# Gate and output stage of a transformer block: transposed squares in ScalarE's queue, output products a product later, another start and end

## The chip, the cores and the metric

The kernel is one program on 1 core of one Trainium2 chip. The metric is device time in microseconds (us); before the change it was 1758.81 us, the median of 3 runs (1757.84 to 1760.7). Beside it stands one profiled execution with a trace of every instruction. Engines are named as in the profile: PE is TensorE's matmul, PEld its weight load, DVE VectorE, ACT ScalarE, POOL GpSimd, SP SyncE. SPq and ACTq rows are an engine's sequencer issuing a DMA. The profile puts "PE" for a matmul and marks the granted clock of TensorE as PEclk.

## What is computed

A pre-norm attention block is followed by a gated MLP; x is 2048 rows of 512, with 32 heads:

```python
h  = x + attention(layernorm(x))                  # 32 heads of 16, softmax
z  = gelu(layernorm(h) @ w_in)                    # 2048 x 1376
z1 = z[:, :688]; z2 = layernorm(z[:, 688:])
g  = w_sp @ z2 + b_sp                             # w_sp is 2048 x 2048, over the rows
y  = h + (z1 * g) @ w_out                         # w_out is 688 x 512
```

The change touches the last two lines only.

## The kernel before

The first 1454 us of the profiled execution are attention, h and z (lines 1 to 1280); the change leaves their instructions alone, but for one small memset on POOL that stands elsewhere. What follows is called the **gate stage** here, lines 1286 to 1565, under a manual schedule: every engine runs its instructions in the order in which the code writes them.

The 2048 output rows are eight pairs of 128-row blocks, p = 0 to 7 (block p and block p + 8). For one p, `w_sp @ z2` is done with seven block products instead of eight, by sums of blocks; they are called b11, t1, t2, b22, t3, b21, n4 after their right operand, and come in that order. Each `product` (line 1299) is 24 matmuls: 8 blocks of 128, each as three fp16 matmuls for fp32 precision (`mm3`, lines 108 to 110). The left operands (256 KB pairs, tile `op`) are fetched eight products ahead from DRAM scratch by SP: `ask`, line 1162, one after every product. Three PSUM tiles A, C, B take the sums:

- A takes b11, is drained by ACT into `p1`, takes t2 on top, is drained by ACT into `v`, takes t3 on top, is read by DVE (`br`), takes n4 on top, is read by DVE (`bl`).
- C takes t1, is drained by ACT into `q5`, takes b22 on top, is read by DVE (`right`).
- B takes b21 and is read by DVE (`left`).

The four pieces of g * z1 (two row blocks, left half and right half of the 688 columns) are put into tile `pr`, multiplied by z1 on POOL (lines 1512, 1520, 1537) or DVE, levelled by a power of two (`level`, DVE; `raise_`, ACT line 1361). "Half 1" is the right columns, ready after t3, "half 0" the left columns, ready after n4.

For the product with w_out, pr has to be transposed. For p = 0 to 6 that is done without PE: DVE transposes 32 x 32 squares within partitions (`squares`, lines 1375 to 1381), SP sends the 384 KB to DRAM scratch (`send`, line 1384), SP brings them back in four DMAs of 96 KB with the squares in their places (`bring`, line 1392), ACT rounds to fp16 (`hi`, line 1398), DVE takes the rest (`lo`, lines 1407 to 1413), and PE multiplies with w_out (`multiply`, line 1437: 16 matmuls of 512 columns for half 1, 18 for half 0, both row blocks). DVE adds the result to h (`gather`, line 1452) and SP stores it (line 1455). The last p transposes on PE instead (`turn`, line 1423; `split`, lines 1431 to 1435).

All this is written out in the loop of line 1480: while p is in its products, the transposed half 1 of p - 1 is multiplied after t1, and its half 0 after b22. Here M1 and M0 stand for these two multiplications. SP's order in a loop turn is: bring of half 1, fetch of z1 and h of the next p (`fetch`, line 1465), operator loads, send and bring of half 0, stores, send of half 1.

At the stage's start SP fetches z1 and h of p = 0, then w_out (`raw_w`, line 1475), and for p = 0 DVE measures w_out's largest entry after t1 (`weigh_w`, line 1321), PE spreads it over the partitions by a matmul with ones after t2 (`measure_w`, line 1327), and ACT and DVE make its fp16 parts (lines 1332 and 1333). The tiles of the stage come from pools `fin_1` and `fin_2`, laid on memory that the pools of the z stage used: a first tile has to wait until the last reader of the old tile under it is done.

Of the kernel before, what the change touches and what calls it, by code (L numbers as in the profile page):

```python
# [19 lines left out]
P = 128  # L20
# [39 lines left out]
def block_kernel(ctx: ExitStack, tc: tile.TileContext, x, wqkv, wo, w_in, w_sp4, b_sp, w_out, out):  # L60
# [1225 lines left out]
    with ExitStack() as fin:  # L1286
        f1 = fin.enter_context(tc.tile_pool(name="fin_1", bufs=1))
# [49 lines left out]
        class Rows:  # L1337
# [45 lines left out]
            def send(self, half):  # L1383
                nc.sync.dma_start(t_scr[2 * (self.p % 2) + half],
                                  self.turned[half].rearrange("p q w i a -> p (q w i a)"))

            def bring(self, half):

                t = self.turned[half] = f2.tile([P, 4, 2, 3, 32], F32, name="whole")
                src = t_scr[2 * (self.p % 2) + half].rearrange("(j b) (q c) -> q b j c", j=4, q=4)  # L1390
                for q in range(4):
                    nc.sync.dma_start(t[32 * q:32 * q + 32].rearrange("b j w i a -> b j (w i a)"), src[q])
# [66 lines left out]
        def fetch(p):  # L1459

            got = []
            for name, src, n in (("z1", z_scr, FH), ("h", h_scr, D)):
                for i in range(2):
                    t = f2.tile([P, n], F32, name=f"{name}{i}", bufs=2 + (name == "h"))
# [4 lines left out]
        with tc.manual_schedule(engines={E.PE, E.Activation, E.DVE, E.Pool, E.SP}):  # L1469
# [4 lines left out]
            nxt = fetch(0)  # L1474
            nc.sync.dma_start(raw_w[:, :5, :], w_out[:5 * P, :].rearrange("(i p) c -> p i c", p=P))
            for r0 in (TW - fn, P - fn):
                nc.sync.dma_start(raw_w[r0:r0 + fn, 5, :], w_out[5 * P:, :])
            now = None
            for p in range(HB):
# [5 lines left out]
                p1, v, q5 = [f2.tile([P, FC], F32, name=n) for n in ("p1", "v", "q5")]  # L1485
# [3 lines left out]
                product(A, "b11")  # L1489
                if p:  # L1490
                    before.send(0)
                nc.scalar.activation(p1, A, AF.Identity, bias=bt)  # L1492
                product(C, "t1")
                nc.scalar.activation(q5, C, AF.Identity, bias=bb)
# [10 lines left out]
                if p:  # L1505
                    for w in range(2):
                        before.gather(1, w, accs[w])
                else:
                    measure_w()
# [20 lines left out]
                if last:  # L1530
                    for w in range(2):
# [65 lines left out]
```

## Time and profile before

| | us |
|---|---|
| median of 3 runs | 1758.81 |
| profiled execution | 1767.72 |
| its span, first to last instruction | 1765.94 |
| gate stage, first b11 matmul (1454.36) to the span's end | 311.58 |
| PE busy in the gate stage | 270.12 |
| DVE, ACT, POOL busy in it | 111.03, 48.63, 32.55 |

The stage is read by loop turns: a turn runs from the first matmul of its b11 to the first of the next one. A row of a stretch table reads: stretch, its length, busy time and number of instructions of each engine, granted clock of TensorE, share of the DMA engines, GB/s. A row of a timeline reads: start, duration, engine, line, operation, out<-in, shape, count, and in brackets the engine's idle time before it and what ended it. A row of the waits reads: who, for whom, total, how often, longest. In the chain a row of a DMA runs from its issue to its landing.

### The profile page before, as it was taken

To read this page: it belongs to the slowest core of one execution; us is meant where nothing else is said; L and a number is where in the kernel's file an instruction comes from. 1 tells how busy PE (TensorE), PEld (TensorE's weight loads), DVE (VectorE), ACT (ScalarE), POOL (GpSimd) and SP (SyncE) were. 2 spreads that over 40 slices of the span, in tenths; PEclk is the share of its full clock that TensorE was granted. 3 is DMA by queue.
4 is the path that set the end of the run, shared out by engine and by line. 5 is a ranking of instruction groups with operands and counts; after the bars stand their busy time and mean duration, and the time that the engine had idled before them with its cause. 6 is when DMAs were issued, how large, how long until landed. Compare 5 with 4: busy or idle time off the path is not lost.

```text
span 1765.9 us, 36677 instructions
## 1 busy us (share of the span) xinstructions
PE 1713.9 (97%) x13499; PEld 645.4 (37%) x13499; DVE 1450.7 (82%) x3051; ACT 1317.7 (75%) x2584; POOL 813.5 (46%) x1062
## 2 busy tenths in 40 slices
PE   9999999999999999999999999999999997988998
PEld 4433222222222222222222222222246664545554
DVE  7688999999999999999999999999567873323334
ACT  4335999999999999999999999999965452111111
POOL 1322777766760388667776776000026762000000
PEclk9999999999999999999999999999999998999999
DMA  5534333332320244435444344001145535656461
GB/s 179 159 101 141 92 87 86 100 92 61 103 50 19 70 123 120 135 109 144 138 123 132 115 140 107 13 13 32 38 118 146 171 132 194 210 167 205 159 196 47
DMA packets 194013, 201.53 MB, mean 114 GB/s; under 512 B 66824, under 2 KB 142920, under 8 KB 193832
## 3 DMA queue, kind: packets, MB, share of 16 engines
q1 hardware_dynamic: 191528, 193.54, 38.2%
q10 hardware_dynamic: 2304, 5.64, 0.8%
q8 instruction: 106, 1.74, 0.4%
q14 instruction: 75, 0.61, 0.1%
HBM read 127.61 MB, written 71.44 MB: 113 GB/s over the span
## 4 chain that ended last, share of the span: by engine, by line
PE 70%; DVE 15%; DMA 6%; POOL 2%; issue 2%; ACT 2%; SPq 2%; ACTq 0%; DVEq 0%; POOLq 0%
PE pv L829 25%; PE s L804 17%; PE m L224 9%; DVE mx L229 7%; PE acc L108 3%; PE acc L110 3%; PE acc L109 3%; PE g L108 3%; PE g L110 3%; PE g L109 3%; DMA t_scr<-squares 2%; DMA rc<-r_scr 2%; DVE ab L238 1%; DVE og L839 1%; DVE rs_t L125 1%
## 5 line engine op out<-in xcount | busy, mean ns | idle before, releaser
L813 ACT ACTIVATE pt<-s 128x512 f32<-128x512 f32 x1968 | 1006.2, 637 | 4.9 <-PE m L224 3.7
L229 DVE TENSOR_REDUCE mx<-m 128x1 f32<-128x512 f32 x1510 | 947.8, 683 | 12.6 <-PE m L224 3.9
L804 PE MATMUL s<-qst,kst 50*128 50x512 f16 x2048 | 604.3, 379 | 0.2
L829 PE MATMUL pv<-pt,vst 128*32 128x256 f32 (+1 forms) x6056 | 598.1, 466 | 4.1 <-DVE og L839 1.3
L224 PE MATMUL m<-kst,qst 48*128 48x512 f16 x1510 | 452.5, 381 | 0.0
L804 PEld LDWEIGHTS <-kst 50*128 50x128 f16 x2048 | 132.0, 94 | 352.0 <-issue 322.9
L829 PEld LDWEIGHTS pv<-pt,vst 128*32 128x32 f32 x6056 | 119.5, 108 | 290.1 <-issue 276.7
L224 PEld LDWEIGHTS <-qst 48*128 48x128 f16 x2048 | 159.2, 93 | 173.7 <-issue 124.5
L224 PE MATMUL m<-uvs,qst 48*128 48x512 f16 x504 | 190.5, 380 | 0.0
L238 DVE CUSTOM_DVE_ANT_0 ab<-m,ab 128x512 f32<-128x512 f32 x252 | 170.7, 677 | 2.7 <-ACT ab L234 2.7
L246 POOL TENSOR_SCALAR nm<-nm 128x16 f32<-128x16 f32 x32 | 6.5, 204 | 359.8 <-DVE nm L243 359.8
L234 ACT ACTIVATE ab<-m 128x512 f32<-128x512 f32 x252 | 157.3, 624 | 16.5 <-PE m L224 15.8
L1361 ACT ACTIVATE pr<-pr,up 128x304 f32<-128x304 f32 (+1 forms) x32 | 17.0, 574 | 138.8 <-DVE up L1315 138.8
L990 POOL TENSOR_TENSOR op<-raw,op 128x512 f16<-128x512 f32 x80 | 92.7, 1159 | 6.1
L913 POOL TENSOR_TENSOR raw<-raw 128x512 f32<-128x512 f32 (+1 forms) x84 | 83.1, 989 | 6.7
L918 POOL TENSOR_TENSOR acc_sp<-acc_sp,raw 128x512 f32<-128x512 f32 x63 | 80.3, 1275 | 4.5
L108 PE MATMUL acc<-wi,hT 128*128 128x344 f16 x256 | 79.1, 309 | 1.4 <-ACT hT L99 1.4
L110 PE MATMUL acc<-wi,hT 128*128 128x344 f16 x256 | 79.1, 309 | 0.3 <-DVE hT L105 0.3
L109 PE MATMUL acc<-wi,hT 128*128 128x344 f16 x256 | 79.1, 309 | 0.0
L1512 POOL TENSOR_TENSOR pr<-pr,z 128x344 f32<-128x344 f32 x8 | 9.7, 1215 | 143.4 <-issue 81.4
L108 PE MATMUL g<-t,op 128*128 128x344 f16 x192 | 60.6, 316 | 4.4 <-ACT p L1492 4.4
L910 POOL TENSOR_SCALAR raw<-raw 128x512 f32<-128x512 f32 (+1 forms) x88 | 52.1, 592 | 19.7 <-DMA raw<-in_wqkv 12.4
(247 smaller groups left out, 2247.4 us busy)
## 6 DMA issues: line engine op xcount, KB each, us to landing
raw<-in_w_sp SPq DMA_DIRECT2D x128, 256.0 KB
s_scr<-op SPq DMA_DIRECT2D x64, 256.0 KB
op<-s_scr SPq DMA_DIRECT2D x32, 512.0 KB
a_scr<-op SPq DMA_DIRECT2D x48, 256.0 KB
op<-a_scr SPq DMA_DIRECT2D x24, 512.0 KB
o_scr<-og SPq DMA_DIRECT2D x64, 128.0 KB
qst<-q_scr SPq DMA_DIRECT2D x192, 32.0 KB
kst<-k_scr SPq DMA_DIRECT2D x48, 128.0 KB
```

Of the source, the lines that this page charges most:

```text
L108: nc.tensor.matmul(ps, lh, rh, start=first, stop=False, **kw)
L109: nc.tensor.matmul(ps, lh, rl, start=False, stop=False, **kw)
L110: nc.tensor.matmul(ps, ll, rh, start=False, stop=last, **kw)
L224: nc.tensor.matmul(acc, q[r, p, c], keys[r, p], start=True, stop=True)
L229: nc.vector.reduce_max(at(t, e if t else e - 1), acc, axis=AX.X)
L234: nc.scalar.activation(ab[0], acc, AF.Abs)
L238: nc.vector.tensor_tensor_reduce(ab[0], acc, ab[0], 0.5, LOW, ALU.add, ALU.max, at(0, 0))
L804: nc.tensor.matmul(s, kst[hg % 2][r, p, kb * P:(kb + 1) * P], qst[hg * NQ + qb][r, p, :], start=True, stop=True)
L813: nc.scalar.activation(pts[p, kb][:, t, :], s, AF.Exp, scale=scales_[hg // 2])
L829: nc.tensor.matmul(pv[0][32 * j:32 * j + 32, a:b], vst[hg % 2][:, c:c + 32], pts[j % 2, kb][:, j // 2, a:b], start=kb == 0, stop=kb == NB - 1,
L913: pool.tensor_mul(got[0] if n else acc, got[0], got[0])
L990: chores.append((lambda: pool.tensor_sub(t[0][:, 1], of(), t[0][:, 0]), TT))
```

## The change

Four things are changed; line numbers of the code after are two higher from line 1286 on.

**Memory.** `p1`, `v`, `q5` and the fetched z1 and h come from two new pools, `fin_0` and `fin_z`, which are opened ahead of the others and so lie at the lowest addresses, where the weights of the earlier stages lay. `raw_w` is loaded ahead of the first fetch. `squares` and `whole` have one buffer for each half instead of two that they share.

**Queue.** `send` and `bring` are issued by ACT instead of SP. Half 1 is sent as soon as it is transposed and before b21, half 0 right at the end of its turn; half 1 is brought after the next turn's p1, half 0 after its q5.

**Order in the turn.** M1 stands after b22 instead of t1, M0 after t3 instead of b22, with their hi, lo and gather. `measure_w` stands after b22.

**Order at the end.** Level of half 0 ahead of the splits of half 1; the two row blocks of M1 apart, with PE's transposes of half 0 between them.

```diff
+        f0 = fin.enter_context(tc.tile_pool(name="fin_0", bufs=2))
+        fz = fin.enter_context(tc.tile_pool(name="fin_z", bufs=2))
         f1 = fin.enter_context(tc.tile_pool(name="fin_1", bufs=1))
...
-                t = self.turned[half] = f2.tile([P, 4, 2, 3, 32], F32, name="squares")
+                t = self.turned[half] = f2.tile([P, 4, 2, 3, 32], F32, name=f"squares{half}", bufs=1)
...
             def send(self, half):
-                nc.sync.dma_start(t_scr[2 * (self.p % 2) + half],
+                nc.scalar.dma_start(t_scr[2 * (self.p % 2) + half],
...
-                    nc.sync.dma_start(t[32 * q:32 * q + 32].rearrange("b j w i a -> b j (w i a)"), src[q])
+                    nc.scalar.dma_start(t[32 * q:32 * q + 32].rearrange("b j w i a -> b j (w i a)"), src[q])
...
-            nxt = fetch(0)
             nc.sync.dma_start(raw_w[:, :5, :], w_out[:5 * P, :].rearrange("(i p) c -> p i c", p=P))
...
+            nxt = fetch(0)
...
                 product(A, "b11")
-                if p:
-                    before.send(0)
                 nc.scalar.activation(p1, A, AF.Identity, bias=bt)
+                if p:
+                    before.bring(1)
                 product(C, "t1")
                 nc.scalar.activation(q5, C, AF.Identity, bias=bb)
                 if p:
                     before.bring(0)
-                    before.hi(1)
-                    before.lo(1)
-                    before.lower(1, 0, 1)
-                    accs = [before.multiply(1, w) for w in range(2)]
...
                 product(A, "t2", False)
                 nc.scalar.activation(v, A, AF.Identity, bias=bt)
                 if p:
-                    for w in range(2):
-                        before.gather(1, w, accs[w])
+                    before.hi(1)
+                    before.lo(1)
+                    before.lower(1, 0, 1)
+                    before.lower(0, 0, 1)
                 product(C, "b22", False)
                 nc.vector.tensor_add(right, C, v)
                 nc.gpsimd.tensor_mul(right, right, z1t[:, FC:])
                 if p:
+                    accs = [before.multiply(1, w) for w in range(2)]
+                    for w in range(2):
+                        before.gather(1, w, accs[w])
                     before.hi(0)
                     before.lo(0)
-                    before.lower(0, 0, 1)
-                    accs = [before.multiply(0, w) for w in range(2)]
+                else:
+                    measure_w()
                 product(A, "t3", False)
...
                 if p:
+                    accs = [before.multiply(0, w) for w in range(2)]
                     for w in range(2):
                         before.gather(0, w, accs[w])
                         before.store(w)
                 if not last:
                     now.squares(1)
+                    now.send(1)
                 product(B, "b21")
...
                 product(A, "n4", False)
-                if not last:
-                    now.bring(1)
...
                     now.squares(0)
+                    now.send(0)
+            accs = [now.multiply(1, 0)]
             now.turn(0, 0)
             now.split(0, 0)
-            now.lower(1, 0, 1)
+            accs.append(now.multiply(1, 1))
+            now.turn(0, 1)
+            now.gather(1, 0, accs[0])
+            now.split(0, 1)
+            now.gather(1, 1, accs[1])
             now.lower(0, 0, 1)
```

In the middle of the stage, ACT's instructions of one turn (p = 2, with the halves of p = 1 coming back) stood so; p, q and v are the drains of A, C, A, pT the fp16 parts of a half that came back, pr the levelled half:

```order
L1492 ACTIVATE p_23658<-g,fig_1847 128x344
L1494 ACTIVATE q_23660<-g,fig_1847 128x344
L1398 ACTIVATE pT_23721<-whole 128x768
L1504 ACTIVATE v<-g,fig_1847 128x344
L1398 ACTIVATE pT_23804<-whole 128x768
L1361 ACTIVATE pr<-pr,up_23859 128x304 x2
L1361 ACTIVATE pr<-pr,up_23937 128x384 x2
```

The same turn of ACT after the change:

```order
L1492 ACTIVATE p_23660<-g,fig_1847 128x344
L1394 DMA whole_23690<-t_scr 32x4x192 x4
L1496 ACTIVATE q_23662<-g,fig_1847 128x344
L1394 DMA whole_23722<-t_scr 32x4x192 x4
L1502 ACTIVATE v<-g,fig_1847 128x344
L1400 ACTIVATE pT_23754<-whole_23690 128x768
L1400 ACTIVATE pT_23812<-whole_23722 128x768
L1363 ACTIVATE pr<-pr,up_23845 128x304 x2
L1386 DMA t_scr<-squares_23876 128x768
L1363 ACTIVATE pr<-pr,up_23938 128x384 x2
L1386 DMA t_scr<-squares_23945 128x768
```

Ten DMA issues a turn stand among ACT's activations now, and both fp16 roundings stand behind all eight brings and behind v. With what they wait for, the bring of half 0 and its neighbours of that turn read:

```order
L1496 ACTIVATE q5_23662<-g_23658,fig2_1847 128x344 [waits PE_49]
L1394 DMA whole0_23722<-t2_scr_85 32x4x192 [waits DMAHW1_49,DMAHW0_49,Activation_49]
L1394 DMA whole0_23722<-t2_scr_85 32x4x192 [waits DMAHW2_49]
L1394 DMA whole0_23722<-t2_scr_85 32x4x192 [waits DMAHW3_49]
L1394 DMA whole0_23722<-t2_scr_85 32x4x192 [waits DMAHW4_49]
L1502 ACTIVATE v_23661<-g_23657,fig2_1847 128x344 [waits PE_49]
```

DMAHW0 to DMAHW7 are eight semaphores that the program hands to all its DMAs in turn, whichever engine issues them; a DMA waits until the one that had its semaphore before has landed. Followed through the program, the first of these four waits for the send of half 0 and for the operator load that SP issues when n4 is done, the second for the operator load that SP issues when b11 is done, the last two for brings of half 1; the brings of half 1 wait in the same way for the send of half 1 and for the fetches of z1 and h of the next p.

On PE, at the same place, M1 stood behind t1 (t_0_20674 is t1's operand, pT the transposed half, wu the parts of w_out):

```order
L110 MATMUL g<-t_0_20674,op 128x344
L108 LDWEIGHTS pT_23421
L108 MATMUL acc<-wu_23065,pT_23421 128x512
L109 LDWEIGHTS pT_23421
L109 MATMUL acc<-wu_23066,pT_23421 128x512
```

and stands behind b22 now:

```order
L110 MATMUL g<-b_0_20672,op 128x344
L108 LDWEIGHTS pT_23454
L108 MATMUL acc<-wu_23071,pT_23454 128x512
L109 LDWEIGHTS pT_23454
L109 MATMUL acc<-wu_23072,pT_23454 128x512
```

Two products, t2 and b22, are now between t1 and M1, and M0 has M1 and t3 between it and b22.

At the stage's start SP's queue read (op is an operator load, h and z the fetches of p = 0 and p = 1):

```order
L1162 DMA op<-a_1_scr 128x2048
L1465 DMA z_23073<-z_scr 128x688
L1465 DMA z_23075<-z_scr 128x688
L1465 DMA h_23077<-h_scr 128x512
L1465 DMA h_23079<-h_scr 128x512
L1475 DMA raw_w<-in_w_out 128x5x512
L1477 DMA raw_w<-in_w_out 48x512 x2
L1465 DMA z_23084<-z_scr 128x688
```

and reads now:

```order
L1162 DMA op<-a_1_scr 128x2048
L1476 DMA raw_w<-in_w_out 128x5x512
L1478 DMA raw_w<-in_w_out 48x512 x2
L1467 DMA z_23082<-z_scr 128x688
L1467 DMA z_23084<-z_scr 128x688
L1467 DMA h_23086<-h_scr 128x512
L1467 DMA h_23088<-h_scr 128x512
L1467 DMA z_23090<-z_scr 128x688
```

The four fetches of p = 0 have gone behind w_out. Before, the first fetch and the first p1 waited for POOL's last instruction of the z stage (n of line 1196), whose tile lay under theirs; now raw_w waits for the last matmul of the z stage, the two 48-row pieces also for a memset of POOL, which now stands behind the t1 parts of block 7, and p1 for loads and stores of the h stage and for its own b11.

More of the change, by code (lines that the diff above doesn't have):

```diff
@@ L1528, in block_kernel @@
                     now.squares(1)
+                    now.send(1)
                 product(B, "b21")
-                if last:
-                    for w in range(2):
-                        now.turn(1, w)
-                        now.split(1, w)
-                else:
-                    now.send(1)
                 nc.vector.tensor_add(left, B, p1)
@@ L1539, in block_kernel @@
                     now.level(0, 0)
+                    for w in range(2):
+                        now.turn(1, w)
+                        now.split(1, w)
+                    now.lower(1, 0, 1)
                     now.raise_(0, 0)
                 product(A, "n4", False)
-                if not last:
-                    now.bring(1)
                 nc.vector.scalar_tensor_tensor(bl, A, bb, z1b[:, :FC], op0=ALU.add, op1=ALU.mult)
@@ L1551, in block_kernel @@
                     now.squares(0)
+                    now.send(0)
+            accs = [now.multiply(1, 0)]
             now.turn(0, 0)
             now.split(0, 0)
-            now.lower(1, 0, 1)
-            now.lower(0, 0, 1)
-            accs = [now.multiply(1, w) for w in range(2)]
-            for w in range(2):
-                now.gather(1, w, accs[w])
-            now.turn(0, 1)
-            now.split(0, 1)
+            accs.append(now.multiply(1, 1))
[3 more added lines that the diff above has]
+            now.gather(1, 1, accs[1])
+            now.lower(0, 0, 1)
             acc = now.multiply(0, 0)
```

10 lines of the change are left out of this document (4 added, 6 removed).

## Prediction

> **What bounds the kernel now.** First the page, for the engine that is busy; then a table of the gate stage by loop turns; then the waits of that stretch; last the timeline around the longest waits. The page's first part says that PE is the bound:
>
> ```profile
> PE 1713.9 (97%) x13499; PEld 645.4 (37%) x13499; DVE 1450.7 (82%) x3051; ACT 1317.7 (75%) x2584; POOL 813.5 (46%) x1062
> ```
>
> So the change can gain only what PE idles, or runs at a lower clock, in the gate stage. The stretches by turn (p = 0, 1, 2, 5, 6, 7; the second number is the length, PEclk the fourth from the end):
>
> ```profile
> 1454.36:1496.74 42.38, 30.13 (x173) 18.63 (x170) 15.62 (x38) 8.29 (x14) 12.36 (x17) 0.80 0.55 186
> 1496.74:1531.44 34.70, 32.22 (x205) 19.52 (x202) 12.25 (x29) 5.33 (x9) 3.38 (x3) 1.00 0.60 179
> 1531.44:1571.54 40.10, 35.27 (x205) 20.06 (x203) 12.34 (x29) 5.32 (x9) 2.72 (x3) 0.91 0.54 175
> ...
> 1643.61:1681.04 37.43, 34.07 (x204) 19.87 (x202) 13.05 (x29) 5.32 (x9) 2.73 (x3) 0.95 0.58 188
> 1681.04:1716.54 35.50, 32.39 (x205) 19.44 (x202) 12.27 (x29) 5.43 (x9) 3.34 (x3) 1.00 0.62 198
> 1716.54:1765.94 49.40, 41.45 (x250) 23.96 (x247) 20.91 (x51) 8.18 (x15) 1.97 (x3) 0.99 0.19 62
> ```
>
> What a turn would take without waits comes from the spacing of matmuls in PE's timeline: three of a product in 0.44 us, and fifteen steps of a multiplication in 3.23 us.
>
> ```profile
> 1730.81 0.31 PE L108 MATMUL g<-t,op 128*128 128x344 f16 x1
> ...
> 1731.25 0.31 PE L108 MATMUL g<-t,op 128*128 128x344 f16 x1
> ...
> 1753.81 0.38 PE L108 MATMUL acc<-wu,pT 128*128 128x512 f16 x1
> ...
> 1757.04 0.38 PE L1447 MATMUL acc<-wu,pT 128*128 128x512 f16 x1
> ```
>
> A product (24 matmuls) is 3.50 us; M1 (16) is 3.45, M0 (18) 3.88. A full turn is 7 x 3.50 + 3.45 + 3.88 = 31.8 us, that of p = 0, without M1 and M0 but with the matmul of measure_w (0.4), 24.9. The six turns p = 1 to 6 took 1716.54 - 1496.74 = 219.8 us: 28.8 over 191.0. Turn p = 0 is 17.5 over. The waits say where:
>
> ```profile
> PE acc L108 <- ACT pT L1398: 18.6, 11, 3.4
> ...
> ACT p L1492 <- POOL n L1196: 6.5, 1, 6.5
> ...
> PE acc L110 <- DVE pT L1407: 5.2, 6, 1.1
> PE g L108 <- ACT p L1492: 4.4, 1, 4.4
> ...
> PE tp L1327 <- issue: 7.9, 1, 7.9
> ```
>
> M1 and M0 wait for hi and lo of halves that have just come back; p = 0 waits for the first p1 (held by POOL's last n), and again for measure_w. The rest of the excess is the clock: 0.80 in p = 0, 0.91 in p = 2, 0.95 in p = 5.
>
> **The turn, p = 1 to 6.** Let t be the time since a turn's first b11 matmul. With M1 behind b22 it is due at t = 14.0, M0 at 20.95. In turn p = 2 (1531.44) DVE, ACT and SP stood so:
>
> ```profile
> 1531.64 0.58 DVE L1544 SCALAR_TENSOR_TENSOR pr<-g,fig,z 128x344 f32<-128x344 f32 x1 [1.29 <-PE g L110]
> 1533.98 1.12 ACT L1361 ACTIVATE pr<-pr,up 128x384 f32<-128x384 f32 x2 [5.32 <-DVE up L1315]
> 1535.13 0.98 DVE L1381 STREAM_TRANSPOSE squares<-pr 128x768 f32<-128x768 f32 x1 [1.25 <-ACT pr L1361]
> 1538.70 0.55 ACT L1494 ACTIVATE q<-g,fig 128x344 f32<-128x344 f32 x1 [2.95 <-PE g L110]
> 1539.01 0.38 SPq L1384 DMA_DIRECT2D t_scr<-squares  x1
> ```
>
> The squares of half 0 are ready at t = 4.7 and were sent at 7.6, behind the fetches in SP's queue; ACT can send at 4.8. Half 1 goes some 4 us before the turn begins, so its bring waits for nothing but the fetches. What decides is the bring of half 0: on ACT, v and both hi stand behind it, and right, M1 and lo behind those. It waits for its send and, by the semaphore that it shares, for the operator load that SP issues when b11 is done (t = 3.7), behind four fetches and one more load. How long a DMA takes in this place the trace shows on the sends, three behind fetches and a load, one behind a load and two stores (4.70), and one with nothing ahead, whose bring followed 2.7 us later:
>
> ```profile
> 1539.01 9.79 DMA t_scr<-squares
> ...
> 1651.27 7.83 DMA t_scr<-squares
> ...
> 1679.58 4.70 DMA t_scr<-squares
> ...
> 1690.04 6.92 DMA t_scr<-squares
> ```
> ```profile
> 1721.69 0.38 SPq L1384 DMA_DIRECT2D t_scr<-squares  x1
> 1724.37 1.73 SPq L1392 DMA_DIRECT2D whole<-t_scr  x4
> ```
>
> So the operator load lands at t = 10.6 (6.92) to 13.5 (9.79). Then come three more issues (a quarter of the 1.73 above is 0.43 each), v (0.55, as q's row) and hi of half 1:
>
> ```profile
> L1398 ACT ACTIVATE pT<-whole 128x768 f16<-128x768 f32 x14 | 11.7, 838 | 17.5 <-DMA whole<-t_scr 17.5
> 1590.36 2.20 DMA whole<-t_scr
> ```
>
> That is 3 x 0.43 + 0.55 + 0.84 + 0.1 = 2.8: M1 can begin at 13.4 to 16.3, against 14.0. The bounds of the new wait are 0 and 2.3 a turn, or 3.8 if the send itself takes 9.79 from 4.8 (it lands at 14.6, and with four issues behind it M1 begins at 17.8). From the row in the middle, 7.83, M1 begins at 14.3 and its third matmul waits about 0.4 for lo: I take **0.8**, in five turns. In p = 1 I take **3**: the fetches there start later, since p = 0 ends late (below). Sum 7, bounds 0 and 23. M0 has room: half 0 lands 2.2 after its last issue, near t = 15, and hi and lo (0.84, 0.95) end near 17 of 20.95. While ACT stands in the bring, nothing else needs it but v, which right needs at 14.2 and t3 at 17.4; SP loses the sends and brings and is only earlier. Ten issues of some 0.4 us on ACT lie in its idle time (5.3 us busy of 34.7).
>
> The Trainium skill, "DMA: Bandwidth & Descriptors", section "Rules for kernel authors", speaks against the queue's part: spreading DMAs over several engines' queues gives no bandwidth, since all run on the same 16 DMA engines. The rows show that the wait in the queue, not the bandwidth, made 2.7 into 9.79; if the rule's bandwidth held here, the wait would be the 2.3 of the upper bound, and the sum 22 instead of 7.
>
> **The clock.** A wait costs more than itself where the clock falls. In p = 5 two short ones did it; the row behind them has 0.63 us in place of 0.38:
>
> ```profile
> 1663.69 0.39 PE L108 MATMUL acc<-wu,pT 128*128 128x512 f16 x1 [0.84 <-ACT pT L1398]
> ...
> 1665.39 0.39 PE L110 MATMUL acc<-wu,pT 128*128 128x512 f16 x1 [1.09 <-DVE pT L1407]
> ...
> 1666.97 0.63 PE L109 MATMUL acc<-wu,pT 128*128 128x512 f16 x1
> ```
>
> Its price is what the clock of 0.95 took from that turn: 0.05 x 37.43 = 1.9 us. With one wait of 0.8 a turn I add nothing; the far bound is 1.9 in each of six turns, 11. "TensorE: Matmul & The Clock Gate", section "What's actually happening", of the Trainium skill says that the clock halves after an idle window of about 3.4 us; by that, waits of 0.84 and 1.09 would be free of it, and the far bound 0; the row says otherwise, and it stands.
>
> **The start, p = 0.** The first fetch went out when POOL was done, w_out behind it, and its maxima began 9.3 us after its issue:
>
> ```profile
> 1465.31 0.80 SPq L1465 DMA_DIRECT2D z<-z_scr  x2
> 1467.10 0.43 SPq L1475 DMA_DIRECT2D raw_w<-in_w_out  x1
> 1476.36 3.65 DVE L1321 TENSOR_REDUCE w<-raw_w 128x1 f32<-128x512 f32 x6 [16.94 <-DMA raw_w<-in_w_out]
> 1481.47 3.78 ACT L1332 ACTIVATE wu<-raw_w,w 128x512 f16<-128x512 f32 x6 [8.63 <-DVE w L1315]
> 1482.22 4.07 DVE L1333 SCALAR_TENSOR_TENSOR wu<-raw_w,w,wu 128x512 f16<-128x512 f32 x6 [0.67 <-ACT wu L1332]
> ```
>
> Now raw_w waits for the z stage's last matmul, near 1454.5. Even with the same 9.3 and 3.65 the maxima are done at 1467.5; measure_w, behind b22, is due at 1454.36 + 4 x 3.50 + 0.16 = 1468.5. p1 no longer waits for POOL, so t2 follows t1. Both waits go, and the low clock behind them: **17.5**. Next late is DVE: the parts of w_out take 4.8 from ACT's first to DVE's last (1481.47 to 1486.29); if they begin some 1.5 after 1468.5, an estimate, they end near 1474.8, br has read A by 1475.3, and n4 needs A at 1475.9. Every us over that is a us lost; I take 0. It makes half 0 of p = 0 a us later, and the next fetch (which needs POOL's last z1) some 3.
>
> **The end, p = 7.** Its waits:
>
> ```profile
> 1725.13 0.39 PE L108 MATMUL acc<-wu,pT 128*128 128x512 f16 x1 [1.43 <-ACT pT L1398]
> ...
> 1737.33 0.39 PE L110 MATMUL acc<-wu,pT 128*128 128x512 f16 x1 [1.11 <-DVE pT L1407]
> ...
> 1753.42 0.55 PE L1423 MATMUL tp<-ident,pr 128*128 128x128 f32 x3 [1.10 <-ACT pr L1361]
> ```
>
> The first two go as in the other turns, here without fetches in the way. The third goes since M1's first row block, whose split is done by then, fills PE while ACT raises half 0. With the 0.16 by which back-to-back products overlap, **4.1**; the bounds of the last part are 0 and 1.3.
>
> **Sum.** 28.8 + 17.5 + 4.1 - 7 = 43.4 us. The profiled execution (1767.72, its span 1765.94) becomes 1724.3. It is 8.9 above the median of the three runs; the difference is taken over, 1758.81 - 43.4 = 1715.4.
>
> **Rivals.**
>
> 1. The loads land late and the bring holds ACT: 3.8 a turn, 23 in all in place of 7, with the clock falling in one turn in two (6). Gain 50.4 - 29 = 21, time 1737. For it: 9.79 in p = 2. Against: two queues instead of one, and 7.83, 6.92 in the other rows. Chance 0.14.
> 2. The start does not move, because something else holds raw_w or p1 in the new memory: gain 43.4 - 17.5 = 25.9, time 1733. The order of waits in the program speaks against it. Chance 0.03.
> 3. Slower. The same bring as mechanism: all of v, hi, right and M1 stand behind it, and it stands behind SP's loads. It eats the 50.4 when six turns lose 8.4 each, that is when the load lands at t = 19.6, 15.9 us after its issue, 1.6 times the longest row. At 20 us it would be 12.5 and 1.9 for the clock in each of six turns, 86: 1758.8 - 50.4 + 86 = 1794. Chance 0.04.
>
> **Chances and range.** Forecast 0.77 (1708 with no new wait, 1724 with the 2.3 in each turn and a low clock once), rival 1 0.14, rival 2 0.03, rival 3 0.04, within 0.2% 0.02 (gains that cancel). The range leaves out the slower case and the worse half of rivals 1 and 2: 1707 to 1735. A difference of 0.2%, 3.5 us, is about what a measurement of this kernel can tell from none. Faster 0.94, same 0.02, slower 0.04.
>
> **What would show it.** In the profile after: turns p = 2 to 6 of 32 to 33 us; PEclk 1.00 in the whole stage; no wait of PE for p1 or measure_w; the first b11 of p = 1 some 25 us after that of p = 0; M1's first matmul waiting for ACT under 1 us, and ACT's waits before its DMA issues ended by operator loads. Wrong it would be with ACT's v later than t = 13, with br behind w_out's parts holding n4, or with sends that take as long on ACT's queue as on SP's.

## The result, and the profile after

| | before | after |
|---|---|---|
| median of 4 runs, us | 1759.32 (1757.84 to 1760.7) | 1729.18 (1726.03 to 1733.43) |
| ratio of the medians | | 0.983, 95% interval 0.9805 to 0.9856 |
| profiled execution, us | 1767.72 | 1733.43 |
| its span | 1765.94 | 1731.7 |
| turn p = 0 | 42.38 | 24.64 |
| turns p = 1 to 6 | 219.80 | 207.73 |
| turn p = 7, to the span's end | 49.40 | 44.71 |

The change gained 30.1 us; 43.4 were forecast. In the first part of the page of the kernel after, PE is busy 8.5 us less than before:

```profile
PE 1705.4 (98%) x13499; PEld 644.6 (37%) x13499; DVE 1449.7 (84%) x3051; ACT 1318.0 (76%) x2584; POOL 812.9 (47%) x1062
```

The number of matmuls is the same; fewer of them came at half the clock. The stretches by turn, columns as in the prediction (length second, PEclk third from the end, where the prediction miscounted it as fourth), for p = 0 to 3 and 5 to 7:

```profile
1454.62:1479.26 24.64, 24.64 (x172) 16.62 (x170) 14.22 (x35) 8.30 (x14) 11.64 (x17) 1.00 0.90 326
1479.26:1516.20 36.94, 33.75 (x204) 20.03 (x202) 13.47 (x33) 5.44 (x9) 3.66 (x4) 0.95 0.65 199
1516.20:1548.45 32.25, 32.04 (x205) 19.60 (x202) 12.36 (x29) 5.44 (x9) 2.75 (x3) 1.00 0.72 217
1548.45:1587.18 38.73, 34.97 (x205) 20.40 (x202) 12.36 (x29) 5.33 (x9) 2.74 (x3) 0.91 0.60 183
...
1620.05:1652.95 32.90, 32.04 (x204) 19.60 (x202) 12.26 (x29) 5.43 (x9) 2.74 (x3) 1.00 0.70 215
1652.95:1686.99 34.04, 32.04 (x204) 19.60 (x202) 12.27 (x29) 5.43 (x9) 2.75 (x3) 1.00 0.65 192
1686.99:1731.70 44.71, 40.79 (x250) 24.40 (x247) 21.00 (x51) 8.18 (x15) 1.39 (x3) 1.00 0.16 51
```

Turn p = 0 is as long as its work: PE is busy all 24.64 us. Turns 2, 4, 5 and 6 are 32.2 to 34.0, but p = 3 is 38.73 and p = 1 36.94. Together the six are 16.7 over 191.0; 7 were allowed. The waits from 1440 us on name one thing that PE waits for in these turns, and what that waits for:

```profile
ACT v L1502 <- DMA whole<-t_scr: 26.6, 6, 5.8
ACT pT L1400 <- DMA whole<-t_scr: 25.1, 10, 4.6
PE acc L108 <- ACT pT L1400: 10.8, 6, 3.8
```

The last row is M1's first matmul, waiting for hi of half 1, in each of the six turns: 10.8 of the 16.7. The clock behind the two long ones takes 1.9 (36.94 - 31.83 - 3.19 in p = 1) and 3.1 (38.73 - 31.83 - 3.76 in p = 3). What made hi late stands in the chain of waits; its rows for p = 3, 4 and 5:

```profile
1553.15 9.75 DMA t_scr<-squares
...
1565.49 0.84 ACT pT L1400
1566.37 0.61 PE acc L108
...
1593.91 7.29 DMA whole<-t_scr
1601.28 0.85 ACT pT L1400
...
1621.70 5.66 DMA h<-h_scr
1627.39 6.71 DMA whole<-t_scr
1634.18 0.85 ACT pT L1400
```

In p = 3 the forecast's mechanism acted: the send of half 0 took 9.75 us, its bring could be issued only then, and v and hi stood behind it. In p = 4 and 5, and likewise in 1, 2 and 6 (7.84, 6.41 and 7.03 us in the chain), the row ahead of hi is a **bring of half 1**: its last part was issued some 7 to 9 us into the turn and took 6.4 to 7.8 us to land, where one before took 2.20 (the row in the prediction). In p = 5 its last issue had also waited for a fetch of h, by the semaphore that the two share. In all six turns the semaphores cost less than the landing: four issues of 0.43 us would put the last 1.3 us behind the first, and it came 1.5 to 3.0 us behind, so 0.2 to 1.7 us are theirs, an estimate; the landing took 4.2 us or more over the 2.20 of before.

The chain names one cause where two can be late together. In p = 1 it names half 1, but v, behind the bring of half 0, ended just as late:

```profile
1492.52 2.53 ACTq L1394 DMA_DIRECT2D whole<-t_scr  x4
1495.09 0.55 ACT L1502 ACTIVATE v<-g,fig 128x344 f32<-128x344 f32 x1 [5.79 <-DMA whole<-t_scr]
1495.74 0.84 ACT L1400 ACTIVATE pT<-whole 128x768 f16<-128x768 f32 x1
```

By the trace's landing events (when a DMA's semaphore is complete), half 1 had landed 16.46 us into that turn, and v was done at 16.38. In p = 3 it was 15.83 and 17.14. In 2, 4, 5 and 6 v was done 0.5 to 1.6 us before half 1 landed, so there half 1 set M1's wait; v alone would have made it 0.4 us at most, an estimate with hi's 0.84. The two long waits, and with the clock behind them 12 of the 16.7 us, thus had both halves late, and only experiments can tell them apart.

### The profile page after: what moved, and what is told of

Same layout as the page of the kernel before. It is cut to its first block, busy times and chain, and to the rows that moved or that the text cites. A ratio compares the mean times of both kernels' runs of the same rounds, so it can differ in the third digit from the quotient of the medians.

```text
span 1731.7 us, 36651 instructions
## 1 busy us (share of the span) xinstructions
PE 1705.4 (98%) x13499; PEld 644.6 (37%) x13499; DVE 1449.7 (84%) x3051; ACT 1318.0 (76%) x2584; POOL 812.9 (47%) x1062
## 4 chain that ended last, share of the span: by engine, by line
PE 71%; DVE 15%; DMA 6%; POOL 2%; issue 2%; ACT 2%; SPq 1%; ACTq 1%; DVEq 0%; POOLq 0%
PE pv L829 25%; PE s L804 17%; PE m L224 9%; DVE mx L229 7%; PE acc L108 4%; PE acc L110 4%; PE acc L109 4%; DMA whole<-t_scr 2%; PE g L110 2%; PE g L108 2%; PE g L109 2%; DVE ab L238 1%; DVE og L839 1%; DMA rc<-r_scr 1%; DVE rs_t L125 1%
## 5 line engine op out<-in xcount | busy, mean ns | idle before, releaser
L1413 DVE TENSOR_TENSOR pT<-whole,pT 128x256 f16<-128x256 f32 x14 | 5.3, 422 | 73.7 <-ACT pT L1400 73.7
```

## The experiments

Two theories. **A**: the bring of half 1 lands late, because ACT issues it after the fetches of z1 and h and after operator loads, whose bytes are then ahead of it or beside it in the DMA engines. **B**, the forecast's: the bring of half 0 holds ACT, and v, hi and M1 behind it. C, a branch of A: not the bytes, but the semaphores that brings and fetches share.

The kernels ran in three groups, each on one chip beside the kernel before (1762.33, 1761.01 and 1761.81 us there).

| group, kernel | us | ratio to before, interval |
|---|---|---|
| 1, start alone | 1744.61 | 0.9897 (0.988 to 0.9913) |
| 1, queue's part undone | 1717.91 | 0.975 (0.9734 to 0.9766) |
| 1, half 1 brought early | 1727.17 | 0.9806 (0.979 to 0.9822) |
| 1, fetches late | 1718.02 | 0.9749 (0.9733 to 0.9765) |
| 2, after again | 1726.63 | 0.9803 (0.9786 to 0.982) |
| 2, hi of half 1 first | 1729.61 | 0.9821 (0.9804 to 0.9837) |
| 2, queue's part and end undone | 1719.22 | 0.9762 (0.9745 to 0.9778) |
| 2, old order in the turn | 1804.38 | 1.0242 (1.0225 to 1.0259) |
| 3, fetches of h late | 1720.69 | 0.9766 (0.9745 to 0.9788) |
| 3, more fetched | 1750.59 | 0.993 (0.9906 to 0.9953) |
| 3, sends alone on ACT | 1717.47 | 0.9748 (0.9727 to 0.9769) |
| 3, before again (one execution) | 1763.0 | |

**The start alone.** Into the kernel before:

```diff
+        f0 = fin.enter_context(tc.tile_pool(name="fin_0", bufs=2))
+        fz = fin.enter_context(tc.tile_pool(name="fin_z", bufs=2))
...
-            nxt = fetch(0)
             nc.sync.dma_start(raw_w[:, :5, :], ...)
+            nxt = fetch(0)
...
-                else:
-                    measure_w()
                 product(C, "b22", False)
...
                     accs = [before.multiply(0, w) for w in range(2)]
+                else:
+                    measure_w()
```

> The kernel before with the start's part alone: pools fin_0 and fin_z ahead of the others, w_out's load ahead of the first fetch, measure_w behind b22. Queue, order of M1 and M0, and the end are as before. Theory of the forecast: the start is worth 17.5 us by itself, since nothing in turn p = 0 hangs on the other parts; turn p = 0 takes 24.6 to 25 us, PE has no wait for p1 or measure_w, and the time is 1759.3 - 17.5 = 1742 (1739 to 1745). Rival: part of the gain is given back in the turns behind it, since p = 1 then finds its fetches and operator loads later against PE; then turn p = 0 is 25 but turns p = 1 to 7 together are 3 to 8 us longer than the 269.2 of before, and the time is 1745 to 1750.

It gained 17.7 us. The rows are turn p = 0, turns 1 to 6 in one stretch, and p = 1:

```profile
1455.53:1480.16 24.63, 24.63 (x172) 16.62 (x170) 14.22 (x35) 8.31 (x14) 11.63 (x17) 1.00 0.83 304
1480.16:1693.85 213.69, 197.24 (x1215) 117.64 (x1213) 74.61 (x178) 32.23 (x54) 20.94 (x19) 0.98 0.60 196
...
1480.16:1517.31 37.15, 33.87 (x204) 19.95 (x202) 13.37 (x33) 5.32 (x9) 4.30 (x4) 0.95 0.57 178
```

Turn p = 0 has no wait left. Turn p = 1 pays for it with 2.5 us (37.15 against 34.70 before), as the rival had it in part, though the six turns together are not longer. They are 213.69 without any edit to them, not 219.80; that is taken up below.

**The queue's part undone.** Against the kernel after:

```diff
-                nc.scalar.dma_start(t_scr[...
+                nc.sync.dma_start(t_scr[...
-                    nc.scalar.dma_start(t[32 * q:...
+                    nc.sync.dma_start(t[32 * q:...
                 product(A, "b11")
+                if p:
+                    before.send(0)
...
-                    before.bring(1)
...
                 product(B, "b21")
+                if not last:
+                    now.send(1)
...
                 product(A, "n4", False)
+                if not last:
+                    now.bring(1)
...
-                    now.send(0)
```

> The kernel after with the queue's part undone: all sends and brings are issued by SP again, at the places of before (send of half 0 behind b11, bring of half 0 behind t1, send of half 1 behind b21, bring of half 1 behind n4, ahead of the next fetches); order in the turn, start and end stay changed. Theory A: what M1 waits for in the kernel after is the bring of half 1, which stands behind the fetches of z1 and h and behind two operator loads in the DMA engines; the queue's part put it there. Then, with SP's old order, M1 waits for nothing, M0 (due 20.95 us after the turn's b11) waits 0 to 2.4 us in a turn, since half 0 lands near 17 to 21.6, and the time is 1719 to 1735, within 6 us of the kernel after. Theory B (the change's own logic and the forecast's): the wait of the sends in SP's queue made the old excess, so undoing the queue brings most of the 28.8 us of turns 1 to 6 back: 1740 to 1750.

It came out faster than the kernel after, below A's range by a little: the queue's part is a loss. Beside the start alone, on the same chip, it is 26.7 us faster, which is the worth of the order in the turn with that of the end. The stretch holds turns 1 to 6, the next row p = 7:

```profile
1671.00:1716.10 45.10, 40.80 (x250) 24.39 (x247) 21.01 (x51) 8.18 (x15) 1.39 (x3) 0.99 0.15 51
...
1479.97:1671.00 191.03, 191.03 (x1214) 118.59 (x1212) 75.93 (x178) 31.82 (x54) 17.32 (x19) 1.00 0.68 223
```

PE is busy through all 191.03 us, the 191.0 of the prediction. Its timeline of turn p = 4 (1575.49), SP and ACT:

```profile
1575.35 1.74 SPq L1394 DMA_DIRECT2D whole<-t_scr  x4
1577.19 1.11 SPq L1467 DMA_DIRECT2D z<-z_scr  x2
...
1586.69 0.83 ACT L1400 ACTIVATE pT<-whole 128x768 f16<-128x768 f32 x1
1587.76 1.75 SPq L1394 DMA_DIRECT2D whole<-t_scr  x4
1591.30 0.84 ACT L1400 ACTIVATE pT<-whole 128x768 f16<-128x768 f32 x1 [3.78 <-DMA whole<-t_scr]
```

The bring of half 1 goes ahead of the fetches and has landed at 1579.2 by the trace's landing events, 3.7 us into the turn; hi runs right behind v. The bring of half 0 is issued 12.3 us into the turn, no earlier than in most turns of the kernel after, and its hi is still done at 16.7 of 20.95. ACT does not wait in it here, though, so what B names is gone as well as what A names.

**Half 1 brought early**, its bring still on ACT:

```diff
-                    before.bring(1)
...
                     now.level(0, 0, 1)
+                    now.bring(1)
                     now.raise_(0, 0, 1)
```

> The kernel after with one step moved: the bring of half 1 stands in ACT's order ahead of the raise of half 0, at the end of its own turn, and so ahead of the next fetches, in place of behind the next turn's p1. Theory A (the bring of half 1 lands late behind the fetches and operator loads): M1's waits for hi of half 1, 10.8 us in the profile of the kernel after with some 4 us of low clock behind two of them, fall to 0 to 3 us; turns p = 2 to 6 take 32.0 to 32.5; the time is 1729 - 10 = 1719 (1715 to 1723). Theory B (the forecast's: the bring of half 0, which stands ahead of v and hi on ACT, decides): M1 waits as before, for v's place in the queue, and the time is 1727 to 1731.

The time does not tell it from the kernel after, and A's 1715 to 1723 was missed. The profiled execution (1723.97, the fastest of the four) shows a wait gone and another in its place:

```profile
PE g L108 <- ACT p L1492: 3.4, 1, 3.4
PE acc L108 <- ACT pT L1400: 1.5, 2, 0.8
```

M1's wait fell from 10.8 to 1.5, as A has it. The two that are left, 0.83 us in p = 2 and 0.68 in p = 4, are B's: half 1 had landed 6.8 and 6.4 us into the turn, and v, behind the bring of half 0, was done at 14.2 and 14.1. And a new wait came, t2 of turn p = 1 for p1. The chain there:

```profile
1482.34 4.31 DMA z<-z_scr
1486.68 0.31 ACTq L1394
...
1487.09 1.13 ACT pr L1363 x2
...
1489.65 0.56 ACT p L1492
```

The bring's last issue waited for a fetch of z1 with the same semaphore, and the raise of half 0, its send and p1 stood behind. What the three executions without a profile, 3 to 5 us longer, waited for is open.

**Fetches late.** The kernel after with one line moved behind b22; in SP's order the fetches then follow t2's operator load:

```diff
-                nxt = None if last else fetch(p + 1)
...
                 product(C, "b22", False)
+                nxt = None if last else fetch(p + 1)
```

> The kernel after with one step moved: the four fetches of z1 and h for the next turn (1.2 MB) stand in SP's order behind the operator load that follows t2, some 10.6 us into the turn, in place of the turn's start. Theory A (traffic in the first 12 us of a turn makes the bring of half 1 and the send of half 0 slow): the bring of half 1 lands within 5 us of its issue in place of 6 to 10, hi of half 1 waits only for v's place, M1's waits fall to 0 to 3 us in all, and the time is 1715 to 1723. Theory B (the bring of half 0 holds ACT, by its place and its shared semaphores): the send still takes its time behind the operator loads, v and hi stand behind it, and the time is 1726 to 1732. The fetches could also collide with the bring of half 0; then M0 waits for hi of half 0, which the kernel after shows nowhere.

A was right: all of PE's waits for hi are one of 0.4 us.

```profile
PE acc L108 <- ACT pT L1400: 0.4, 1, 0.4
```

Sends and brings are on ACT here as in the kernel after, bring of half 0 ahead of v and all; only the fetches' bytes ahead of them are gone. The sends of half 0 in turns 2 to 6 land 3.9 to 4.3 us after their issue, against 5.7 to 9.8 in the kernel after (landing events of both traces). The last part of the bring of half 1 still takes 4.4 to 6.3 us, more than the expected 5 in three turns, with operator loads and the send still beside it; it lands as late as 13.6 us into a turn, so the margin is thin. The halves are not told apart here: v, behind the bring of half 0, is done earlier too, at 11.3 to 13.5 us in place of 12.9 to 17.1.

**The kernel after again**, for the second group's chip:

> The kernel after, unchanged, beside the next three on one chip, so that the price of the queue's part can be read without the difference between chips (the kernel before measured 1759.3 and 1762.3 us on two). Theory A (the bring of half 1 lands behind the fetches): its waits differ from execution to execution with the landings, M1 waits 6 to 15 us for hi of half 1 in all, and the time is 1726 to 1733, 8 to 15 us over the kernel with the queue's part undone. Theory B (nothing but the landing of half 0): the same time, but the waits would follow the landing of the send of half 0.

It took 1726.63. In this profile M1's waits are

```profile
PE acc L108 <- ACT pT L1400: 6.9, 5, 3.1
```

and turns 1 to 6 take 200.23 us, 9.2 over 191.0, against 16.7 in the first profile. The waits follow the landings of half 1: in p = 2, 3, 4 and 6 M1 begins 1.0 us behind them (13.85 to 14.50 us into the turn).

**Hi of half 1 first**, so that B's queue behind the bring of half 0 is gone:

```diff
-                    before.bring(0)
...
                 nc.scalar.activation(v, A, AF.Identity, bias=bt)
                 if p:
                     before.hi(1)
+                    before.bring(0)
                     before.lo(1)
```

> The kernel after with ACT's order in the turn changed: v and hi of half 1 ahead of the bring of half 0, so that neither stands behind it any longer. Theory B (the forecast's step: what decides is the bring of half 0, behind which v, hi and M1 stand): M1's waits go, and the time is 1715 to 1720. Theory A (the bring of half 1 itself lands late): only turns in which the bring of half 0 was late too gain, 1.1 us in p = 3 of the profile of the kernel after and nothing in the others; the time stays within 3 us of the kernel after, and M1 goes on waiting for hi of half 1, whose own wait is ended by a landing of whole.

It gains nothing, 3 us the other way. The waits:

```profile
ACT pT L1400 <- DMA whole<-t_scr: 54.5, 13, 6.5
ACT v L1500 <- PE g L110: 18.1, 8, 3.0
...
PE acc L108 <- ACT pT L1400: 8.8, 5, 4.5
```

v now waits for PE alone, and hi of half 1 still stands there until its half has landed. So the landing of half 1 is enough to make the whole loss, and the bring of half 0 is not needed for it.

**Queue's part and end undone.** The lines of the end as before, on the kernel without the queue's part:

```diff
-            accs = [now.multiply(1, 0)]
             now.turn(0, 0)
             now.split(0, 0)
-            accs.append(now.multiply(1, 1))
...
+            accs = [now.multiply(1, w) for w in range(2)]
```

> The kernel with the queue's part undone, and the order at the end of before put back as well (level of half 0 behind the splits of half 1, both row blocks of M1 in one, PE's transposes of half 0 not between them). The forecast gave this part 1.10 us of PE's wait and some 0.16 of overlap, bounds 0 and 1.3: 1717.9 becomes 1719.2 (1718 to 1719.5), with PE waiting 1.1 us for ACT's raise before a transpose. Rival: the end is worth more, since the last gather and store come earlier too: 1721 or more.

1719.22, as expected, and the wait is back; its last turn is 46.36 against 45.10:

```profile
PE tp L1425 <- ACT pr L1363: 1.2, 1, 1.2
```

Beside the kernel after on the same chip (1726.63) it also prices the queue's part: 7.4 us, and 1.3 more for the end that it lacks, 8.7.

**The old order in the turn**, with the queue's part in place: M1 behind t1 and M0 behind b22 again.

```diff
                     before.bring(0)
+                    before.hi(1)
+                    before.lo(1)
+                    before.lower(1, 0, 1)
+                    accs = [before.multiply(1, w) for w in range(2)]
```

> The kernel after with the order of M1 and M0 in the turn put back (M1 behind t1, M0 behind b22), the queue's part, start and end as after. Both theories let M1 wait here, since it is due 7.0 us into the turn and its half lands at 13 to 16: the queue's part alone should be a loss. M1 waits 6 to 9 us in each of turns 1 to 6, with low clock behind it (1.7 to 3 us each): 45 to 70 us over the kernel with the queue's part undone, 1763 to 1788. Rival (the queue's part pays for itself even with the old order): 1735 to 1745, as with the start alone.

1804.38, beyond the expected 1763 to 1788 and slower than before: the waits are 9 to 11 us a turn, not 6 to 9.

```profile
PE acc L108 <- ACT pT L1400: 60.1, 7, 11.2
```

With M1 and M0 at their old places the queue's part is a loss of some 60 us against the start alone; their later places hide all but some 9 of it.

**Fetches of h late.** As the fetches late, for h alone (0.5 of 1.2 MB):

```diff
-                nxt = None if last else fetch(p + 1)
+                nxt = None if last else fetch(p + 1, ("z1",))
...
                 product(C, "b22", False)
+                if not last:
+                    nxt += fetch(p + 1, ("h",))
```

> The kernel after with a part of the fetches moved: the two fetches of h for the next turn (0.5 of 1.2 MB) stand in SP's order behind the operator load that follows t2, those of z1 stay at the turn's start. Theory A (the bring of half 1 lands late because of the bytes that stand ahead of it in the DMA engines): the two fetches of h landed 1.4 us apart from those of z1 in turn p = 4 of the profile of the kernel after, so the bring lands some 1.4 us earlier; M1's waits of 3.1, 0.7, 0.8, 1.0 and 1.3 us (the second profile of the kernel after) become 1.7 and four times 0, and the time is 1719 to 1723, between the kernel after (1727) and the one with all four fetches moved (1718). Theory C (not the bytes, but the brings' semaphores shared with the fetches): the semaphores are shared with operator loads and stores here too, and the time stays at 1725 to 1730.

1720.69, inside A's range; of PE's waits for hi one is left, in p = 1:

```profile
PE acc L108 <- ACT pT L1400: 2.3, 1, 2.3
```

In that one the bring of half 0 was last: half 1 had landed 15.19 us into the turn, and hi stood behind v, which was done at 15.68.

**More fetched**, the other way:

```diff
                     got.append(t)
+            if p > 1:
+                for i in range(2):
+                    t = raw_w.rearrange("p i c -> p (i c)")[:, i * FH:(i + 1) * FH]
+                    nc.sync.dma_start(t, z_scr[rows(p, i), :])
             return got
```

> The kernel after with more bytes fetched at the start of turns 1 to 6: the two row blocks of z1 of the next turn are fetched a second time, behind h, into the tile of w_out's raw entries, which nothing reads any more (0.7 MB a turn more; nothing is left out). Theory A (bytes ahead of the bring of half 1): it lands 2 us or more later in each of six turns, M1 waits 2 us or more longer in each, with low clock behind the longer waits: 12 to 22 us over the kernel after, 1739 to 1749. Theory C (semaphores, not bytes): the order of the brings in ACT is unchanged and the time stays within 4 us of the kernel after.

1750.59, some 22 us over the kernel after by the two ratios (0.993 and 0.9803) and a little above A's range. The waits show that C has a share too:

```profile
PE g L108 <- ACT q L1500: 12.2, 5, 2.6
PE acc L108 <- ACT pT L1400: 8.7, 4, 2.6
PE g L108 <- DMA op<-s_scr: 3.6, 1, 3.6
```

Next to M1's waits, b22 waits for q5 in five turns: on ACT q5 stands behind the bring of half 1, whose later issues wait until the longer row of fetches has landed. So bytes ahead decide, first by the landing, then by ACT's standing in the issue. Bytes and semaphores are not fully separated: a DMA that is added or moved also changes which of the later ones share a semaphore.

**Sends alone on ACT:** the brings back on SP, half 1 behind n4.

```diff
-                    nc.scalar.dma_start(t[32 * q:...
+                    nc.sync.dma_start(t[32 * q:...
-                if p:
-                    before.bring(1)
...
                 product(A, "n4", False)
+                if not last:
+                    now.bring(1)
```

> The kernel after with half of the queue's part undone: the sends stay in ACT's queue at their new places, the brings are issued by SP again (half 1 behind n4, ahead of the next fetches; half 0 behind t1). Theory A (the place of the bring of half 1 behind the fetches costs the time, not the engine that sends): no wait of PE for hi, 1717 to 1720, as with the whole queue's part undone. Rival: the sends on ACT cost too (raise and p1 stand beside them), or SP, which waits in the bring of half 1 for a send that lands 4.4 us after its issue, fetches z1 and loads operators too late: 1722 to 1730, with a wait of PE for op or of POOL for z.

1717.47, the lowest of all, and not to be told from the kernel with the whole queue's part undone: the sends' place is worth nothing, and what counts is that the brings are on SP, half 1's ahead of the fetches and half 0's where ACT does not wait in it. Turns 1 to 6:

```profile
1479.31:1670.37 191.06, 191.06 (x1214) 118.59 (x1212) 75.88 (x178) 31.94 (x54) 17.33 (x19) 1.00 0.67 220
```

This kernel and the two at 1718 beat both the kernel before and the kernel after, by 2.5% and some 0.5 to 0.8%.

**Before again:**

> The kernel before, unchanged, for a second profile of it. The forecast was summed from one profiled execution of 1767.72 us, 8.9 us above the median, and took that difference over to the kernel after. Theory: the 8.9 us were waits of that execution, in the very terms that the change removes. Then a second profile, with a time of 1758 to 1764, has turns p = 1 to 6 of some 214 us together (22 to 25 over 191.0) in place of 219.8, and the term of 28.8 was 4 to 6 us too large. Rival: the 8.9 us lie in the first 1454 us or in turn p = 0, and the turns p = 1 to 6 take 218 to 221 again.

1763.0, and the turns p = 1 to 6 in one row:

```profile
1497.06:1711.82 214.76, 197.35 (x1215) 117.57 (x1213) 74.33 (x174) 32.16 (x54) 19.56 (x18) 0.98 0.60 193
```

They are 23.8 over 191.0, not 28.8. The spans of the two profiles differ by 4.7 us (1765.94 and 1761.2), the turns by 5.0. It is one execution, on another chip.

## Why the prediction was right in sign and too large

The time lies inside the range and the change is faster, but it is 13.8 us above the forecast: 1729.18 against 1715.4. Of these, 8.9 are the difference between the profiled execution and the median, carried over (1724.3 became 1715.4), and 4.9 the new wait, which cost 11.9 of the median (1729.18 - 1717.3) in place of 7. By the ratios of the groups it is 9 to 14 us.

1. **What bounds it: right.** A turn's ideal of 31.8 us, from the spacing of matmuls, is what the kernel without the queue's part runs, 191.03 us for six. With no new wait the terms sum to 50.4, and 1767.72 - 50.4 = 1717.3; that kernel takes 1717.91, on a chip where the kernel before was 3 us slower.
2. **The start, 17.5: right.** 17.7 in the two profiles' turns (42.38 and 24.64) and 17.7 by itself in the runs. That the runs give it so closely is in part luck, since p = 1 pays 2.5 in the profile of the start alone. The w_out parts, named as next late, end near the forecast 1474.8; the chain of the kernel after has them on DVE to 1475.0:

```profile
1470.92 4.08 DVE wu L1335 x6
```

   n4 began at 1475.76 with no wait.
3. **The turns, 28.8: mis-sized.** The failed step is "the difference is taken over". The profiled execution was slow in part in the terms that were to be removed: its turns 1 to 6 have 28.8 of excess, a second execution 23.8. A change that removes the waits removes their bad luck too, so the sum belongs to the profile's own time as far as the excess lies in these waits, by the second profile 5.0 of the 8.9; 1724.3 would have been 4.9 off.
4. **The new wait, 7: the wrong step.** "Half 1 goes some 4 us before the turn begins, so its bring waits for nothing but the fetches. What decides is the bring of half 0." Half 1 was costed at nothing, yet it landed last in five of six turns, the last part of its bring 6.4 to 7.8 us long in the chain, and in four of them by 0.5 to 1.6 us. What I overlooked: before, its bring went ahead of the fetches in SP's queue, and now it goes behind them, for ACT issues it only after raise and send of half 0 and p1. What was costed, the bring of half 0, was about the right size: with half 1 out of the way (half 1 brought early) it made M1 wait 0.83 and 0.68 us in two turns, where 0.8 was forecast, and the 3 for p = 1 came as 3.19, with both halves late. But ACT's wait before it was ended by the send of half 0 in all six turns (landed at 10.4 to 14.5 us), not by the operator load (9.8 to 12.5; 10.6 to 13.5 were forecast). Putting the bring of half 0 behind v and hi gained nothing (hi of half 1 first). One sign of being wrong that the prediction names came here, a v later than 13 us: it began at 15.83 and 16.59 in p = 1 and 3.
5. **"The wait in the queue, not the bandwidth": wrong, and it was the part where the Trainium skill had spoken against the change.** Sends of half 0 took as long on ACT's queue (7.1, 5.7, 9.8, 6.3, 6.3 and 6.4 us in turns 1 to 6, landing events) as on SP's (7.1, 9.8, 8.1, 6.2, 7.8 and 6.9); the prediction had listed just that as what would prove it wrong. "DMA: Bandwidth & Descriptors", section "Rules for kernel authors", of the Trainium skill says that another queue gives no bandwidth and saves only issue time. This case agrees. The prediction's price for it, 22 instead of 7, does not come out of the 2.3 a turn that it names: six times 2.3 is 13.8, and 15.7 with one low clock. Measured are 16.7 in the profile and 11.9 at the median, so 13.8 to 15.7 was nearer than 7. With the sends alone on ACT they still took 6.8 to 9.0 us in turns 2 to 6. Taking the fetches away (3.9 to 4.3 us) did what another queue had not.
6. **The clock: missed twice.** PEclk was to be 1.00 all through; it is 0.95 and 0.91 in p = 1 and 3, 5.0 us. Turns of 32 to 33 us were forecast for p = 2 to 6; 2, 4 and 5 are (32.25, 32.87, 32.90). M1 waited under 1 us, as forecast, in the same three; in 1, 3 and 6 it was 3.19, 3.76 and 2.0.
7. **The end, 4.1: right in kind, a little small.** 49.40 became 44.71, so 4.7; the terms that the prediction shows for it sum to 3.8. The last part alone, 1.10 forecast with a bound of 1.3, is 1.3 in the last turn.
8. **The rivals.** Rival 1 (loads late, 1737) was nearer in kind than the forecast, with the late transfer mostly on the other half. Rival 2 (the start does not move) is out by turn p = 0. Rival 3, a bring that eats the gain, exists in kind, again with half 1: with the old order in the turn it does so, at 1804. M1's later place is what kept it off.

## What to carry to other kernels

When a transfer is moved to another engine's queue, list the bytes that were issued behind it and now go ahead of it: here the place in the traffic decided (a landing after 2.2 us or after 6.4 to 7.8), and which queue issued the sends was worth nothing. A step that "has time" needs its landing worked out at its new place as carefully as the step that looks critical. And a profiled execution that is slower than the median may be slow in the very waits that are to go (here by 5.0 of 8.9 us), so a sum of removed waits is taken from its own time, or from a second profile, not from the median.

## What the runs showed of the hardware

The clock falls after shorter waits than one would read from most rows, and not by length alone. After a single wait of 2.61 us in the kernel before (p = 4) it did not:

```profile
1581.31 0.39 PE L108 MATMUL acc<-wu,pT 128*128 128x512 f16 x1 [2.61 <-ACT pT L1398]
1581.53 0.38 PE L109 MATMUL acc<-wu,pT 128*128 128x512 f16 x1
```

After one of 2.16 in the kernel with the start alone it did:

```profile
1489.49 0.43 PE L108 MATMUL acc<-wu,pT 128*128 128x512 f16 x1 [2.16 <-ACT pT L1400]
1489.71 0.63 PE L109 MATMUL acc<-wu,pT 128*128 128x512 f16 x1
```

In all profiles of this study every wait of PE in the gate stage over 3.1 us was followed by half clock (matmuls of 512 columns 0.43 us apart in place of 0.22), waits under 2.1 with no other in the 6 us before them were not, and between these it went both ways. A low phase that began within a run of matmuls lasted 3.4 us (1489.71 to 1493.12 here, 1497.34 to 1500.74 in the kernel after). "TensorE: Matmul & The Clock Gate", section "What's actually happening", of the Trainium skill states a free-running window of about 3.4 us: the length of the low phases agrees, and a free-running window would let equal waits end differently, but the idle window that the section names as what halves the clock is as long, and here a wait of 2.16 us was enough.
